# An attention output product on TensorE: stationary operand in four pieces of 32 columns instead of two of 64

## The chip, the cores and the metric

One core of a Trainium2 chip runs the whole program. The metric is device time in microseconds (us), the median of several executions. The core has a matrix engine (TensorE, PE in the profile, with its weight loads listed apart as PEld), VectorE (DVE), ScalarE (ACT), GpSimd (POOL), and DMA queues that SyncE (SP) feeds.

## The reference

The input is a gated linear attention (an mLSTM) over 4 batches, 8 heads, 768 positions and head dimension 40, whose result goes through two feed-forward networks in sequence:

```python
m_new = np.maximum(f_gate[:, :, t] + m, i_gate[:, :, t])
f_stab = np.exp(f_gate[:, :, t] + m - m_new)
i_stab = np.exp(i_gate[:, :, t] - m_new)
C = f_stab * C + i_stab * einsum('bhd,bhe->bhde', vt, kt)
n = f_stab * n + i_stab * kt
y[:, :, t] = sigmoid(o_gate) * einsum('bhde,bhe->bhd', C, qt) / maximum(abs(n . qt), 1)
...
x = y as 3072 tokens x 320
h = (x @ w1) * (x @ w2) @ w3 @ w_out            # first network, width 1024
out = max(h @ w1', h @ w2', h @ w3') @ w_out'   # second network, width 768
```

(Shortened: sizes of axes that only broadcast are left out.)

## The kernel before

**Attention.** The recurrence is worked in chunks of 88 positions (nine to a sequence, the last one of 64). A *unit* is one batch, one chunk and four of the eight heads: 4 x 9 x 2 = 72 units. For each unit TensorE makes the scores of the chunk (L569 or L594), VectorE and GpSimd turn them into a weight tile `pk`, and `outs` (L621 to L629) multiplies `pk` with `kv`. `pk` is the stationary operand: on its 128 partitions stand the 88 positions of the chunk and 40 rows of carried state, and its 128 columns are the 88 output positions and the 40 rows of the next state. `kv` is the moving operand, 41 columns: 40 values and the normalizer. So one product serves outputs and state update, and its result `o` has 128 partitions. In the last chunk there is no next state: its `pk` has 64 columns. For the first chunk the contraction has 88 rows instead of 128.

Both operands are 32-bit floats, and TensorE does each such matmul of the program in two passes: the profile lists two loads and two matmuls for one `PE.matmul` of `outs`.

`outs` cuts the columns of `pk` at multiples of 64, for each of four heads. The two halves write PSUM partitions 0 to 63 and 64 to 127, that is, they lie in different column ranges of the array. That makes 8 matmuls in a unit (4 in a unit of the last chunk), 16 pairs of load and matmul in the profile (8 in the last chunk). A unit's run of them is called a *group* below.

**The networks.** Blocks of 384 tokens go through products with 384 (or 320) moving columns and 128 x 128 stationary operands: `group` (L702 to L706), `b_step` (L769 to L773), `d_step` (L788), and a fold of two weight matrices at the start (L930).

**The order.** All operations are noted in a list, and `Plan.run` replays them with costs per operation and fixed biases to fix the order of each engine ahead of time. The operation that holds a unit's `outs` has a cost of its own there, 910 ns (500 in the last chunk), which is a number in the code and not derived from the matmuls that it holds. Units are spread among the network's steps from about 80 us on.

After `outs`, VectorE reads the result for the next chunk's state (L634) and for the output (L647 to L650).

Of the kernel before, what the change touches and what calls it, by code (L numbers as in the profile page):

```python
# [280 lines left out]
def mlstm_moe_kernel(  # L281
# [55 lines left out]
    o, where, over, gates_done = 0, {}, {t: [] for t, _ in shared}, {}  # L337
# [30 lines left out]
    def T(*key):  # L368
        return made[key]
# [7 lines left out]
    o = 0  # L377
# [30 lines left out]
    def f():  # L408
# [5 lines left out]
         r=[("g", "ff")], w=[("g", "git")])  # L414

    def f():
# [6 lines left out]
         r=[("g", "git")], w=[("g", "aug", 1)])  # L423
# [55 lines left out]
    def ub(u):  # L479
        b, r = divmod(u, 18)  # L480
        return b, r // 2, r % 2, GL[r // 2], 128 if r > 1 else L
# [41 lines left out]
    def unit(u):  # L523
# [48 lines left out]
        else:  # L572
# [19 lines left out]
            def f():  # L592
                for h in range(4):
                    PE.matmul(T("s", u)[0:L, h], lhsT=ks[:, h], rhs=T("qs", u)[:, h], start=True, stop=True)  # L594
                if duo:
                    outs(u - 1)
# [19 lines left out]
        if u + 1 < DUO or u == NU - 1:  # L616
            new(("o", u), [128, 4, 41], F32, f"ac{u % 3}" if u < 10 else "aq")
            P.op("P", 910 if m > n else 500, lambda: outs(u), cols=210, r=[("pk", u), ("kv", u)], w=[("o", u)])
            rest(u)

    def outs(u):  # L621
        b, c, g, n, r = ub(u)
        m = 128 if c < NCH - 1 else n
        for h in range(4):
            for a in range(0, m, 64):
                PE.matmul(  # L626
                    T("o", u)[a:a + 64, h], lhsT=T("pk", u)[:r, h, a:a + 64], rhs=T("kv", u)[:r, h, 40:81],
                    start=True, stop=True,
                )  # L629

# [516 lines left out]
```

## Time and profile before

| | |
|---|---|
| time, median of 3 runs | 722.54 us (722.18 to 725.04) |
| the profiled execution's own time | 725.08 us |
| its span, first to last instruction | 723.1 us |
| TensorE busy | 682.0 us, 94% of the span |
| weight loads busy | 648.9 us, 90% |
| granted TensorE clock, mean over the span | 0.991 of full speed |

Busy time counts each instruction from its start to its modelled end, so instructions that overlap on TensorE are merged and "busy" does not mean at its peak. The times of the section below come from that one execution.

### The profile page before, as it was taken

The page shows a single profiled execution, that of the slowest core. Times are in us where ns is not written, and L with a number is a line of the kernel's source. Part 1 is how long each engine was busy: PE and PEld are TensorE (multiplying, and loading weights), DVE is VectorE, ACT ScalarE, POOL GpSimd, SP SyncE. Part 2 cuts the span into 40 slices and gives each one's busy share as a digit, 9 for nine tenths or more (in the row PEclk, how much of TensorE's full clock was granted, in tenths as well). Part 3 has the DMA queues.
Part 4 walks back from the last instruction along what each step waited for, and adds up shares of the span by engine and source line. Part 5 has one row for each costly group of instructions (what it writes and reads, how often), then busy time and mean ns, then how long its engine had stood idle before and what let it go on. Part 6 is the DMA issues. An engine that isn't in the chain of part 4 may idle for free.

```text
span 723.1 us, 13690 instructions
## 1 busy us (share of the span) xinstructions
PE 682.0 (94%) x4853; PEld 648.9 (90%) x4853; DVE 437.6 (61%) x998; ACT 373.4 (52%) x697; POOL 306.3 (42%) x438
## 2 busy tenths in 40 slices
PE   1569799999999999999999999999999999999998
PEld 1546788889999999999999999999999999999998
DVE  4668877776776865876366666754747632233333
ACT  5859899689864454554343445645333222231311
POOL 1756774566545646674044447643416200000000
PEclk9978999999999999999999999999999999999999
DMA  7987788465433445453033445432305100000000
GB/s 209 249 220 229 225 251 230 141 187 173 137 104 100 101 117 166 120 147 82 9 87 86 110 119 155 122 83 65 88 2 124 39 1 27 1 1 1 1 28 28
DMA packets 50958, 78.91 MB, mean 109 GB/s; under 512 B 11882, under 2 KB 37930, under 8 KB 50890
## 3 DMA queue, kind: packets, MB, share of 16 engines
q1 hardware_dynamic: 50890, 78.04, 39.9%
q8 instruction: 38, 0.62, 0.4%
q14 instruction: 30, 0.25, 0.1%
HBM read 73.98 MB, written 4.03 MB: 108 GB/s over the span
## 4 chain that ended last, share of the span: by engine, by line
PE 78%; ACT 7%; DMA 6%; DVE 3%; issue 2%; POOL 2%; SPq 1%; POOLq 0%; DVEq 0%
PE wk L702 13%; PE wk L704 11%; PE wk L703 11%; PE ac L788 9%; PE wk L706 6%; PE wk L705 6%; PE ac L769 4%; PE aq L626 4%; PE ac L773 4%; PE ac L771 3%; PE wk L930 2%; ACT stg L874 2%; PE aq L594 1%; PE aq L569 1%; DMA qq<-in_qk 1%
## 5 line engine op out<-in xcount | busy, mean ns | idle before, releaser
L722 DVE TENSOR_TENSOR pl<-pr,ph 128x384 fp32r<-128x384 f32 (+1 forms) x91 | 61.1, 672 | 78.3 <-ACT ph L718 74.5
L718 ACT CAST ph<-pr 128x384 fp32r<-128x384 f32 (+1 forms) x114 | 57.8, 510 | 87.1 <-PE ac L788 46.6
L702 PE MATMUL wk<-xh,wch 128*128 128x384 f32 x288 | 99.7, 346 | 0.0
L704 PE MATMUL wk<-xl,wch 128*128 128x384 f32 x288 | 97.0, 337 | 0.0
L703 PE MATMUL wk<-xh,wcl 128*128 128x384 f32 x288 | 97.0, 337 | 0.0
L753 DVE TENSOR_TENSOR pr<-pr,wk 128x384 f32<-128x384 f32 (+1 forms) x98 | 52.9, 541 | 63.4 <-PE wk L706 58.2
L702 PE MATMUL wk<-xh,wah 128*128 128x384 f32 x256 | 90.8, 355 | 0.0
L722 POOL TENSOR_TENSOR pl<-pr,ph 128x384 fp32r<-128x384 f32 (+1 forms) x23 | 23.7, 1033 | 153.9 <-ACT ph L718 136.7
L703 PE MATMUL wk<-xh,wal 128*128 128x384 f32 x256 | 86.1, 336 | 0.0
L704 PE MATMUL wk<-xl,wah 128*128 128x384 f32 x256 | 86.0, 336 | 0.0
L545 POOL TENSOR_TENSOR dd<-am,dd 128x352 f32<-128x352 f32 (+2 forms) x72 | 55.9, 777 | 54.7 <-DMA dd<-d_na 54.0
L559 POOL TENSOR_TENSOR pk<-kv,dd 128x160 f32<-128x160 f32 (+1 forms) x64 | 37.9, 593 | 66.5 <-PE aq L626 59.3
L735 ACT COPY pr<-wk 128x384 f32<-128x384 f32 x64 | 30.5, 476 | 63.3 <-PE wk L706 63.2
L655 POOL TENSOR_TENSOR misc<-misc 88x160 f32<-88x160 f32 (+1 forms) x62 | 44.4, 715 | 41.6 <-DVE misc L650 37.8
L553 ACT ACTIVATE dd<-dd 128x352 f32<-128x352 f32 (+2 forms) x72 | 35.2, 493 | 51.1 <-POOL dd L549 50.4
L737 DVE TENSOR_TENSOR pr<-pr,wk 128x384 f32<-128x384 f32 x64 | 35.2, 550 | 38.7 <-PE wk L706 32.5
L750 ACT COPY pr<-wk 128x384 f32<-128x384 f32 x48 | 23.2, 483 | 68.4 <-PE wk L706 68.3
L874 ACT ACTIVATE stg<-stg 128x512 f16<-128x512 f32 (+2 forms) x41 | 52.7, 1285 | 4.5 <-DVE stg L866 4.0
L702 PEld LDWEIGHTS wk<-xh,wch 128*128 128x128 f32 x288 | 54.1, 188 | 1.0
L703 PEld LDWEIGHTS wk<-xh,wcl 128*128 128x128 f32 x288 | 54.1, 188 | 0.0
L704 PEld LDWEIGHTS wk<-xl,wch 128*128 128x128 f32 x288 | 54.0, 188 | 0.0
L788 PE MATMUL ac<-wd,ph 128*128 128x320 f32 x288 | 51.4, 313 | 0.0
(133 smaller groups left out, 1683.5 us busy)
## 6 DMA issues: line engine op xcount, KB each, us to landing
misc<-in_qk SPq DMA_DIRECT2D x44, 330.0 KB
dd<-d_na SPq DMA_DIRECT2D x56, 176.0 KB
kv<-in_kv SPq DMA_DIRECT2D x72, 121.5 KB
stg<-in_w3t SPq DMA_DIRECT2D x13, 512.0 KB
stg<-in_wc SPq DMA_DIRECT2D x9, 512.0 KB
qq<-in_qk SPq DMA_DIRECT2D x64, 66.0 KB
misc<-in_og SPq DMA_DIRECT2D x31, 120.0 KB
out<-misc SPq DMA_DIRECT2D x23, 160.0 KB
```

What stands on the lines that cost most here:

```text
L545: P.op("G", 735, lambda: G.tensor_tensor(out=T("dd", u)[:r], in0=am[:r, c, h0:h0 + 4].unsqueeze(2).to_broadcast([r, 4, n]), in1=T("dd", u) ...
L655: P.op("G", 485, lambda: G.tensor_tensor(out=yv(), in0=yv(), in1=sg(b, c).rearrange("p (h d) -> p h d", d=D)[:n, g * 4:g * 4 + 4], op=ALU.mult
L702: PE.matmul(p, lhsT=h_[:, kt], rhs=xh[:, kt], start=kt == 0, stop=False)
L703: PE.matmul(p, lhsT=l_[:, kt], rhs=xh[:, kt], start=False, stop=False)
L704: PE.matmul(p, lhsT=h_[:, kt], rhs=xl[:, kt], start=False, stop=False)
L705: PE.matmul(p, lhsT=r_, rhs=xh[:, 2], start=False, stop=False)
L706: PE.matmul(p, lhsT=r_, rhs=xl[:, 2], start=False, stop=True)
L718: P.op("A", act(n), lambda sl=sl: A.copy(out=T("ph", key)[:, sl], in_=T(*src)[:, sl]), r=[src + part], w=[("ph", key) + part])
L722: e.tensor_tensor(out=T("pl", key)[:, sl], in0=T(*src)[:, sl], in1=T("ph", key)[:, sl].bitcast(F32), op=ALU.subtract)
L753: P.op("V", dve(sl.stop - sl.start), lambda ps=ps, sl=sl: V.tensor_tensor(out=T(*sc)[:, sl], in0=T(*sc)[:, sl], in1=T(*ps)[:, sl], op=ALU. ...
L788: PE.matmul(T(f"ac{m}", (k, 1)), lhsT=src[:, m * 128:m * 128 + 128], rhs=w[:, o:o + DM], start=first_, stop=last_,)
L874: A.activation(out=sign, in_=tl()[:, :, 1].bitcast(F32), func=AF.Copy)
```

## The change

The stationary operand is cut at multiples of 32 instead of 64. Nothing else is edited; in particular the cost that the planner uses for the operation stays.

```diff
         for h in range(4):
-            for a in range(0, m, 64):
+            for a in range(0, m, 32):
                 PE.matmul(
-                    T("o", u)[a:a + 64, h], lhsT=T("pk", u)[:r, h, a:a + 64], rhs=T("kv", u)[:r, h, 40:81],
+                    T("o", u)[a:a + 32, h], lhsT=T("pk", u)[:r, h, a:a + 32], rhs=T("kv", u)[:r, h, 40:81],
                     start=True, stop=True,
                 )
```

A unit has now 16 matmuls (8 in the last chunk) with 32 stationary columns each. The order of TensorE's program shows this at a unit between two stretches of the first network; each row is a matmul's line, output, operands and stationary x moving columns, and x16 counts the program's matmuls:

```order
 L706 MATMUL wk_131<-xl_84,war 128x384
 L569 MATMUL aq_133<-misc 88x88 x4
-L626 MATMUL aq_132<-kv_104,pk_97 64x41 x8
+L626 MATMUL aq_132<-kv_104,pk_97 32x41 x16
 L702 MATMUL wk_129<-xh_81,wah 128x384
 L703 MATMUL wk_129<-xh_81,wal 128x384
```

Nothing moved: the group stands between the same neighbours, and this holds for every group. Of the other engines no instruction changed its place either. The program's matmuls of L626 are 544 before and 1088 after, so the pairs of load and matmul in a profile go from 1088 to 2176.

## Rows read from the trace of the kernel before

**Rows 1.** The page: span, TensorE's two rows, granted clock in 40 slices.

```profile
span 723.1 us, 13690 instructions
...
PE 682.0 (94%) x4853; PEld 648.9 (90%) x4853; DVE 437.6 (61%) x998; ACT 373.4 (52%) x697; POOL 306.3 (42%) x438
...
PEclk9978999999999999999999999999999999999999
```

**Rows 2.** Busy time of each engine in three stretches, then granted clock.

```profile
0.00:100.00 100.00, 64.84 (x506) 53.82 (x507) 70.08 (x160) 77.59 (x118) 59.07 (x93) 0.93 0.83 227
100.00:600.00 500.00, 497.34 (x3645) 475.58 (x3644) 327.85 (x764) 266.56 (x518) 243.71 (x342) 1.00 0.41 110
600.00:723.00 123.00, 119.79 (x706) 119.52 (x704) 39.69 (x75) 29.21 (x63) 3.51 (x4) 1.00 0.03 11
```

**Rows 3.** The chain that ended last, by engine and by line (the page).

```profile
PE 78%; ACT 7%; DMA 6%; DVE 3%; issue 2%; POOL 2%; SPq 1%; POOLq 0%; DVEq 0%
PE wk L702 13%; PE wk L704 11%; PE wk L703 11%; PE ac L788 9%; PE wk L706 6%; PE wk L705 6%; PE ac L769 4%; PE aq L626 4%; PE ac L773 4%; PE ac L771 3%; PE wk L930 2%; ACT stg L874 2%; PE aq L594 1%; PE aq L569 1%; DMA qq<-in_qk 1%
```

**Rows 4.** That chain in order of time: start, us, what.

```profile
104.88 0.60 PE aq L626 x16
...
116.14 0.59 PE aq L626 x8
...
306.03 1.98 issue
308.05 0.78 POOL dd L545
308.82 0.90 POOL qs L579
...
584.56 0.59 PE aq L626 x8
```

**Rows 5.** Groups by line and shape: matmuls and loads (xcount, busy us, mean ns).

```profile
L626 PE MATMUL aq<-kv,pk 128*64 128x41 f32 x832 | 37.2, 233 | 2.4 <-DVE misc L650 1.7 <-DVE xl L684 0.5
...
L626 PEld LDWEIGHTS aq<-kv,pk 128*64 128x64 f32 x832 | 30.6, 137 | 8.8 <-issue 2.8 <-DVE misc L650 2.0 <-DVE xl L684 1.1
...
L569 PEld LDWEIGHTS aq<-misc 40*88 40x88 f32 x144 | 12.6, 154 | 8.8 <-issue 2.6 <-DVE pk L610 2.5 <-DVE kv L634 1.7
```

**Rows 6.** Timeline of the weight loads around one full group: start, us, what, xcount.

```profile
168.15 0.19 PEld L706 LDWEIGHTS wk<-xl,war 128*128 128x128 f32 x1
168.59 0.55 PEld L626 LDWEIGHTS aq<-kv,pk 128*64 128x64 f32 x16 [0.25 <-issue]
169.18 0.19 PEld L702 LDWEIGHTS wk<-xh,wah 128*128 128x128 f32 x1
```

**Rows 7.** The last pair of that group: timeline of narrow windows, loads, then matmuls.

```profile
168.99 0.14 PEld L626 LDWEIGHTS aq<-kv,pk 128*64 128x64 f32 x2
...
169.02 0.24 PE L626 MATMUL aq<-kv,pk 128*64 128x41 f32 x2
```

**Rows 8.** Timeline of the loads around a group of the last chunk.

```profile
277.98 0.54 PEld L626 LDWEIGHTS aq<-kv,pk 128*64 128x64 f32 x8
278.56 0.19 PEld L702 LDWEIGHTS wk<-xh,wah 128*128 128x128 f32 x1
```

**Rows 9.** Timelines of two score products L569: 88 stationary columns, moving columns 88, then 64.

```profile
159.13 0.70 PEld L569 LDWEIGHTS aq<-misc 40*88 40x88 f32 x8 [0.25 <-issue]
...
159.13 0.85 PE L569 MATMUL aq<-misc 40*88 40x88 f32 x8
...
111.97 0.70 PEld L569 LDWEIGHTS aq<-misc 40*88 40x88 f32 x8 [0.25 <-issue]
...
111.97 0.83 PE L569 MATMUL aq<-misc 40*88 40x64 f32 x8
```

**Rows 10.** Timelines of folds L930 (32-bit floats, 320 moving columns): one matmul, then 16.

```profile
114.94 0.43 PE L930 MATMUL wk<-wof,w 128*128 128x320 f32 x1
...
159.92 4.58 PE L930 MATMUL wk<-wof,w 128*128 128x320 f32 x16
```

**Rows 11.** Loads of a group at the lower clock, 53.9 to 55.0 us.

```profile
53.94 0.94 PEld L626 LDWEIGHTS ac<-kv,pk 128*64 128x64 f32 x16 [0.20 <-issue]
```

**Rows 12.** DMA queues that fetch instructions (the page, part 3).

```profile
q8 instruction: 38, 0.62, 0.4%
```

## The prediction

> **What bounds the kernel now.** I read the page first. TensorE is busy 94% of a 723.1 us span and its clock is at 0.9 or more in all slices but one [rows 1]. By stretches the picture is sharper: from 100 to 600 us TensorE is busy 497.34 of 500 us, while VectorE has 328 and ScalarE 267 [rows 2]. Before 100 us it is busy only 64.84 of 100, so there it waits for others. The chain that ended last says the same: 78% of it is TensorE [rows 3]. So a microsecond taken from TensorE after 100 us shortens the kernel, unless a wait appears that TensorE's work had covered.
>
> Then the part that changes. In the page's list of the chain L626 has 4% [rows 3]. In the chain in order of time I count 54 of the 72 groups: 46 with x16, which take 0.60 us each, and 8 with x8, which take 0.59 [rows 4]; all but one lie after 100 us. That is 46 x 0.60 + 8 x 0.59 = 32.3 us of chain, and it bounds any gain. The other 18 groups lie beside other work, mostly in the first 100 us.
>
> **How a group spends its 0.60 us.** A group of x16 is eight waves (four heads, two passes), each of two pairs of load and matmul that go to the two column halves. From the loads' row: 0.55 us from the first start to the last end, one load takes 137 ns [rows 5, 6], the second of a wave starts under 10 ns after the first (two loads together take 0.14 us, two matmuls 0.24 [rows 7]; I take 7 ns). So seven intervals between waves take 550 - 137 - 7 = 406 ns: **58 ns a wave**. The remaining 600 - 406 = 194 ns are the last wave and the way to the next group's first load at 169.18 [rows 6]; they do not depend on how often the wave before was repeated.
>
> A group of the last chunk shows what a second column tile costs: it has one pair in a wave, and its eight loads take 0.54 us, (540 - 137) / 7 = 58 ns a wave again [rows 5, 8]. Twice the pairs, in two column ranges, cost the same wave and 0.01 us a group (0.60 against 0.59 [rows 4]). Pairs in different column ranges run side by side.
>
> What sets the 58 ns? Not the matmuls' 41 columns. The score products have 88 stationary columns, and eight of their loads take 0.70 us whether 88 or 64 columns move [rows 9]: (700 - 154) / 7 = 78 ns in both [rows 5]. So with 64 columns moving the stationary side sets the interval, and between 64 and 88 stationary columns it rises by 20 ns for 24 columns, 0.83 ns a column. At the lower clock the same 16 loads take 0.94 us [rows 11]; with a load of 137 to 270 ns that is 95 to 114 ns a wave. The interval follows TensorE's clock, so a queue that hands out instructions at a rate of its own is not what sets it now.
>
> **The change part by part.**
> - *Loads of 32 columns.* By the slope the load side of a wave falls to 58 - 32 x 0.83 = **31 ns**. No row shows a load under 64 columns. Lower bound 31; upper bound 58, if something other than the columns holds it there.
> - *The matmul under it.* The moving side then comes next. The nearest row is the fold, also 32-bit floats: 16 in 4.58 us, one in 0.43, so (4580 - 430) / 15 = 277 ns for 320 columns [rows 10], 0.86 ns a column, so 35 ns for 41. The score product with 88 moving columns needs 78 ns by either side, about 3 ns over 0.86 x 88. I take **38 ns** a wave.
> - *Twice as many pairs.* A wave has four pairs in four column ranges. If each starts 7 ns after the one before, the fourth starts 21 ns after the first and all four fit in 38 ns. The last wave ends 14 ns later than now (7 ns in the last chunk, where one pair becomes two).
> - *Entry and exit.* Before a group the loads sit idle (0.25 us, put down to issue [rows 6]) and behind it the next load comes about 0.19 us after the last wave's. The group has the same neighbours, so both stay.
> - *Instructions.* 1088 more pairs, 2176 more instructions on 13690 [rows 1]. Their fetching is a queue that moves 0.62 MB and takes 0.4% of the DMA engines' time [rows 12]; a fifth more is hidden under a core whose DMA engines are busy 41% after 100 us [rows 2]. Without that cover it would be a stall ahead of some groups; a bound is 0.4% x 723 x 0.2, 0.6 us.
> - *Readers.* VectorE reads `o` after the last matmul, as now, only sooner.
>
> A full group gains 7 x (58 - 38) - 14 = 126 ns, one of the last chunk 140 - 7 = 133 ns. On the chain: 46 x 0.126 + 8 x 0.133 = **6.9 us**. Some comes back: at 306 us the chain leaves TensorE for GpSimd and an issue gap [rows 4], and there are a few such places; TensorE's idle time from 100 to 600 us is 2.7 us [rows 2], and when it runs 7 us ahead these waits grow. I take back about a sixth, 1.1 us, and keep **-5.8 us**. Against the profiled execution's own 725.08 us that is 719.3; on the median of the three runs, which is 2.5 us lower, 722.54 - 5.8 = **716.8 us**. For a reader to weigh other values: each ns on the wave is 7 x 54 = 0.38 us of the kernel. The wave at which nothing changes is 58 - 14/7 = 56 ns.
>
> What a measurement of this kernel can tell from no change is about 0.5%, 3.6 us, that is 67 ns a group: faster by that much needs a wave of 46 ns or less, slower by that much one of 66 ns or more.
>
> **The rivals.**
>
> *The wave does not shrink.* In the last pair the loads start at 168.99 and the matmuls at 169.02 [rows 7]: the matmul follows its load by some 30 ns, and the next load follows that matmul by another 28. If these are fixed lags and not parts of a load's 64 columns, a wave stays at 58 ns and each group loses 14 ns: +0.8 us, 723.3. For it: no row has a load this short. Against it: the interval does grow from 64 to 88 columns. Waves from 47 to 65 ns, by whatever cause, belong here.
>
> *Four are too many at once (the case that ends slower).* The rows show two column ranges side by side, never four. For the second pair to start, its load has to go ahead of the first pair's matmul, which still waits. If only one waiting matmul can be passed, pairs three and four start when the first two are through: a wave becomes two half waves of 38 ns, 76 in all, and the last pair ends 45 ns after the first, against 7 now. A group then costs 7 x 18 + 38 = 164 ns more, +8.9 us on 54 groups: 731.4. It decides from a wave of 66 ns on. For it: twice the pairs in the same queue, and nothing in the trace that is denser than two starts in 58 ns. Against it: from one pair to two, the whole price was 0.01 us a group.
>
> *Each matmul has a least spacing.* If a matmul cannot start less than 25 ns after another on average, a wave of four takes 100 ns, and its last start comes 75 ns after the first: 7 x 42 + 68 = 362 ns a group, +19.5 us, 742. The rows speak for neither side fully: two starts come under 10 ns apart [rows 7], but the mean over a group is 29 ns, which such a limit would allow. The Trainium skill, page "TensorE: Matmul & The Clock Gate", section "Wait — 56ns, not 53.3ns?", states this limit: start to start never drops below about 25 ns however small the moving operand. By that rule the time is the 742 of this rival. The pairs under 10 ns apart disagree with it as a limit for different column ranges, so it gets the smallest chance.
>
> The Trainium skill's page "TensorEngine Tiling (Array Packing)", section "Instruction Overhead", also warns against taking the tiling factor from a dimension that is already small, since a matmul with one moving column takes as long as one with 60. Here the cut is in the stationary columns, and rows 9 show the stationary side setting the interval. If a matmul of 41 columns cost as one of 60, the moving side would be 52 ns at the fold's 0.86 ns a column instead of 35, and the estimate by that page is a gain of some 1.5 us, inside the first rival.
>
> **How the numbers follow.** Forecast (wave 31 to 46 ns) 0.52, its own range 713.5 (31 ns, nothing given back: 7 x 27 - 14 = 175 ns a group, 9.4 us) to 719. The wave does not shrink 0.24, around 723. Four are too many 0.15, around 731. Least spacing 0.09, around 742. The median is that of the likeliest, 716.8. The range from 713.5 to 732 leaves out the last rival and little else. Faster 0.51 (the forecast, but for runs in which the waits eat it); same 0.26; slower 0.23 (the last two).
>
> **What would show it.** In the profile after: L626 with x2176 on TensorE, a full group's 32 loads in about 0.27 + 0.13 = 0.40 us instead of 0.55, the next product 0.47 us after the group's first load instead of 0.60, and the half groups alike; TensorE busy in L626 after 100 us falling by some 7 us, and the idle time between 100 and 600 us up by about a microsecond. I would be wrong if a wave lasts 56 ns or more, which the same row tells; or if the groups shrink and the span does not, and then a wait for GpSimd, ScalarE or a DMA stands in the chain where L626 stood. A change of the clock in the first 100 us, where 0.93 was granted [rows 2], could hide or feign a few us; the clock row tells that apart.

## The result

The changed kernel takes 716.74 us (median of 4 runs, 715.74 to 717.16) against 723.13 us for the kernel before, now with one run more (4 runs, 722.18 to 725.04). The ratio is 0.9906, 95% interval 0.9882 to 0.9930: faster by 6.8 us, between 5 and 8.5. The prediction said 716.8. That is closer than its reasons deserve. It forecast a gain of 5.8 us on a lower median (722.54), and two of its terms were wrong in opposite directions: a group gained 29% more than forecast, and 46 groups counted instead of 54.

The page of the profile after, with the lines that answer to [rows 1, 3, 12] (the profiled execution took 715.74 us):

```profile
span 713.5 us, 15876 instructions
...
PE 672.9 (94%) x5941; PEld 638.5 (89%) x5941; DVE 438.5 (61%) x998; ACT 372.6 (52%) x697; POOL 306.5 (43%) x438
...
PEclk9978999999999999999999999999999999999999
...
q8 instruction: 47, 0.77, 0.5%
...
PE 75%; ACT 8%; DMA 6%; DVE 4%; POOL 3%; issue 2%; SPq 2%; POOLq 0%; ACTq 0%; DVEq 0%
```

There are 1088 pairs of load and matmul more, TensorE's busy time is 9 us shorter, and the chain that ended last has given up 3 points of TensorE, mostly to ScalarE, VectorE and GpSimd. The clock row reads the same. The span is 9.6 us shorter while the medians differ by 6.4: the profiled execution of before took 725.08 us, more than any of the four timed ones, and some 2 us of the difference between the two traces lie ahead of 105 us. The runs' own spread covers that: one of the runs below, with TensorE's program as before up to there, reaches the same group as early.

The stretches, to set beside [rows 2]:

```profile
100.00:600.00 500.00, 496.38 (x4557) 474.74 (x4556) 328.33 (x768) 266.51 (x520) 242.29 (x340) 1.00 0.42 110
```

TensorE's idle time from 100 to 600 us went from 2.7 to 3.6 us. So it is as full as it was, and it finishes earlier.

The loads around the group that answers to [rows 6], then the one of the last chunk that answers to [rows 8] (start, us, what, xcount):

```profile
167.55 0.38 PEld L626 LDWEIGHTS aq<-kv,pk 128*32 128x32 f32 x32 [0.25 <-issue]
167.98 0.19 PEld L702 LDWEIGHTS wk<-xh,wah 128*128 128x128 f32 x1
...
275.72 0.37 PEld L626 LDWEIGHTS aq<-kv,pk 128*32 128x32 f32 x16
276.14 0.19 PEld L702 LDWEIGHTS wk<-xh,wah 128*128 128x128 f32 x1
```

One load takes 110 ns now:

```profile
L626 PEld LDWEIGHTS aq<-kv,pk 128*32 128x32 f32 x1664 | 21.1, 110 | 9.3 <-DVE misc L650 3.1 <-issue 1.9 <-DVE xl L684 1.2
```

The reader reads a wave from it as before: (380 - 110 - 20) / 7 = **36 ns** (predicted 38, before 58). From the group's first load to the next product's it is 167.98 - 167.55 = **0.43 us** (predicted 0.47, before 0.60), and 0.42 in the last chunk. The idle 0.25 us ahead of the group is unchanged.

### The profile page after: what moved, and what is told of

Same layout as the page of the kernel before. It is cut to its first block, busy times and chain, and to the rows that moved or that the text cites. A ratio compares the mean times of both kernels' runs of the same rounds, so it can differ in the third digit from the quotient of the medians.

```text
span 713.5 us, 15876 instructions
## 1 busy us (share of the span) xinstructions
PE 672.9 (94%) x5941; PEld 638.5 (89%) x5941; DVE 438.5 (61%) x998; ACT 372.6 (52%) x697; POOL 306.5 (43%) x438
## 4 chain that ended last, share of the span: by engine, by line
PE 75%; ACT 8%; DMA 6%; DVE 4%; POOL 3%; issue 2%; SPq 2%; POOLq 0%; ACTq 0%; DVEq 0%
PE wk L702 13%; PE wk L703 12%; PE wk L704 12%; PE ac L788 9%; PE wk L706 6%; PE wk L705 6%; PE ac L769 4%; PE ac L773 4%; PE aq L626 3%; ACT stg L874 3%; PE ac L771 3%; DMA kv<-in_kv 2%; DMA stg<-in_wo 2%; PE aq L594 2%; DMA stg<-in_w3t 2%
## 5 line engine op out<-in xcount | busy, mean ns | idle before, releaser
L655 POOL TENSOR_TENSOR misc<-misc 88x160 f32<-88x160 f32 (+1 forms) x62 | 42.5, 685 | 44.4 <-DVE misc L650 39.7
```

Source lines behind the costliest of these rows:

```text
L655: P.op("G", 485, lambda: G.tensor_tensor(out=yv(), in0=yv(), in1=sg(b, c).rearrange("p (h d) -> p h d", d=D)[:n, g * 4:g * 4 + 4], op=ALU.mult
```

## What the experiments asked

The theory is that of the prediction: a wave lasts as long as the slower of two sides, the loads (0.83 ns for each stationary column, and 5) and the moving columns (0.86 ns each, and 1 to 3), and pairs in different column ranges run side by side. The rivals: stationary columns alone set the wave; the way in and out of the divided array is what counts; the order in the queue does not matter. A second question is where along the kernel a shorter group counts. Six of the runs have one timed execution each (both with 81 moving columns, the pieces of 21 and 20, the two orders of the queue, both widths in one group). They are read by their traces; a difference of one or two us between their times shows nothing.

**No cut, 128 columns.** (Below, only the loop in `outs` is edited where nothing else is said; lines with - are those of the changed kernel.)

```diff
-            for a in range(0, m, 32):
-                PE.matmul(T("o", u)[a:a + 32, h], lhsT=T("pk", u)[:r, h, a:a + 32], ...)
+            PE.matmul(T("o", u)[:m, h], lhsT=T("pk", u)[:r, h, 0:m], ...)
```

> The operand is not cut at all: one matmul of 128 stationary columns a head (64 in the last chunk). Theory (a wave lasts as long as the slower of its load side, 0.83 ns a stationary column and 5, and its moving side, 0.86 ns a moving column; column ranges run side by side): a wave of 0.83 x 128 + 5 = 112 ns, seven intervals 0.78 us, and since the array is not divided the loads need not sit idle before and behind a group; a group with its way in and out some 0.2 us longer than with two of 64, about 11 us on 54 groups: 733 us (728 to 738). Rival (the way in and out of the divided array is what costs, and waves stay near 58 ns): a gain of 0.2 us a group, about 712.

730.41 us, ratio to before 1.0097 (1.0059 to 1.0135): 7 us slower. The loads of a full group:

```profile
225.29 0.97 PEld L625 LDWEIGHTS aq<-kv,pk 128*128 128x128 f32 x8
226.19 0.19 PEld L701 LDWEIGHTS wk<-xh,wch 128*128 128x128 f32 x1
```

With 192 ns for one load, (970 - 192) / 7 = 111 ns a wave, against 112 by the line through 64 and 88 columns. There is no idle time ahead of the group, but that pays back only a part. So the load side is shown at 64, 88 and 128 columns, and the rival with the way in and out is out.

**81 moving columns**, with four of 32 and with two of 64. The product takes the keys along (`rhs=T("kv", u)[:r, h, 0:81]`, `o` is 81 columns wide), and its readers use the last 41. The run with two of 64 is edited from the kernel before.

> Four of 32 columns, and 81 moving columns instead of 41 (the keys go through the product as well; only the 41 columns used before are read). Theory: the moving side sets the wave now, 0.86 x 81 + 1 to 3 = 71 to 73 ns, where 41 columns gave 36; a full group about 0.25 us longer than in the changed kernel, 13 us in all: about 730. Rival (the wave of 36 ns is set by the 32 stationary columns): 36 ns, 717 us.

> Two of 64 columns, and 81 moving columns instead of 41. Theory: a wave of 71 to 73 ns by the moving side, the same as with four of 32, against 58 by the load side with 41 moving columns; group 0.09 to 0.10 us longer than before, 5 us in all: about 728, and no more than 2 us from the run with four of 32. Rival (stationary columns set the wave): 58 ns, 723 us.

729.76 and 730.32 us. The loads, of four of 32:

```profile
176.36 0.58 PEld L626 LDWEIGHTS aq<-kv,pk 128*32 128x32 f32 x32 [0.25 <-issue]
177.07 0.19 PEld L702 LDWEIGHTS wk<-xh,wah 128*128 128x128 f32 x1
```

and of two of 64:

```profile
174.83 0.62 PEld L626 LDWEIGHTS aq<-kv,pk 128*64 128x64 f32 x16 [0.25 <-issue]
175.55 0.19 PEld L702 LDWEIGHTS wk<-xh,wah 128*128 128x128 f32 x1
```

0.71 and 0.72 us: with 81 moving columns the cut is worth nothing, since the moving side sets both waves. Read as above, a wave is (580 - 110 - 20) / 7 = 64 ns and (620 - 137 - 7) / 7 = 68 ns. That is under the expected 71 to 73 because the first interval of a group is short (29 and 55 ns); from the second on it is 69 to 75 ns in both. That is the other half of the theory, and it puts the limit of this change: it pays as long as the loads are the slower side.

**41 moving columns in two pieces of 21 and 20**, to bring the loads back on top.

```diff
         for h in range(4):
-            for a in range(0, m, 32):
+            for x, y in ((0, 21), (21, 41)):
+                for a in range(0, m, 32):
```

> Four of 32 columns with the moving operand in two pieces of 21 and 20 columns: 64 pairs in a full group, 16 waves. Theory: a wave is set by its loads now, 0.83 x 32 + 5 = 31 to 32 ns, fifteen intervals 0.47 us, the group 0.66 us against 0.43: +12 us, about 729. Rival 1 (the moving side sets it throughout): 20 ns a wave, 0.49 us, about 720. Rival 2 (the 36 ns are four starts of 9 ns each, a limit of the queue): 36 ns a wave, 0.73 us, about 733.

731.77 us, and in the trace:

```profile
175.36 0.64 PEld L627 LDWEIGHTS aq<-kv,pk 128*32 128x32 f32 x64 [0.25 <-issue]
176.03 0.19 PEld L703 LDWEIGHTS wk<-xh,wah 128*128 128x128 f32 x1
```

(640 - 110 - 20) / 15 = 34 ns a wave and 0.67 us a group, against 0.66 by the theory, 0.49 and 0.73 by the rivals. The moving side alone (20 ns) is out. The mean of 34 lies between the loads' 31 and the queue's 36, but the first half of the group tells them apart. Its 32 loads are as many as a whole group of the changed kernel has (there 0.38 us):

```profile
175.36 0.35 PEld L627 LDWEIGHTS aq<-kv,pk 128*32 128x32 f32 x32 [0.25 <-issue]
```

(350 - 113 - 20) / 7 = 31 ns a wave, with 113 ns for one of these loads and four starts in each wave. So the loads set it, and a limit of the queue at 36 ns is out. In the second half the four ranges fall out of step, which makes the mean longer.

**The order of the queue.** The column range outside, the head inside:

```diff
-        for h in range(4):
-            for a in range(0, m, 32):
+        for a in range(0, m, 32):
+            for h in range(4):
```

> The same 32-column matmuls as in the changed kernel, the column range in the outer loop and the head in the inner one, so that the next pairs in the queue go to the same range. Theory: pairs of one range can't overlap and matmuls start in order, so a full group is 32 waves of 31 to 38 ns with one pair each, about 1.2 to 1.3 us instead of 0.43; on 54 groups some 45 us: about 760 us. Rival (the queue pulls later pairs ahead, or fewer columns alone made the gain): the order doesn't matter, 717 us.

737.96 us. The order matters (21 us), but the group is not the 1.2 to 1.3 us of pairs one by one:

```profile
174.69 0.90 PEld L626 LDWEIGHTS aq<-kv,pk 128*32 128x32 f32 x32 [0.25 <-issue]
175.64 0.19 PEld L702 LDWEIGHTS wk<-xh,wah 128*128 128x128 f32 x1
```

0.95 us. The single records show why the theory was too strict: pairs of one range start 36 ns apart, but the next range begins about 180 ns after the first one. Up to that moment, 174.87, six loads and five matmuls have started:

```profile
174.69 0.29 PEld L626 LDWEIGHTS aq<-kv,pk 128*32 128x32 f32 x6 [0.25 <-issue]
...
174.69 0.37 PE L626 MATMUL aq<-kv,pk 128*32 128x41 f32 x5
```

So three of the first range's eight matmuls still wait. (The records do not name the range; from there on two rows of starts run side by side, and the new one is known by its short first interval of 28 ns.) So a range seems to take up to about three waiting pairs, and what stands behind them can go ahead into another range. That gave a test, the same loops for two heads at a time, four pairs in a row instead of eight:

```diff
-        for h in range(4):
-            for a in range(0, m, 32):
+        for g2 in (0, 2):
+            for a in range(0, m, 32):
+                for h in (g2, g2 + 1):
```

> The 32-column matmuls in another order: for two heads at a time, all of one column range before the next, so four pairs in a row go to the same range (eight in a_outer, two in the changed kernel). In a_outer the second range started after 180 ns, with three pairs of the first still to come, and a full group took 0.95 us instead of 1.2 to 1.3. Theory: a range can hold about three waiting pairs, so four in a row let all ranges run side by side and the group takes 0.43 to 0.48 us, as in the changed kernel: 717 to 720 us. Rival (ranges overlap only at the seams between runs of the same range, in proportion to the runs' length): 0.6 to 0.7 us, about 727 to 731.

714.03 us (one run; its first 90 us were 2 to 3 us shorter than in the trace of the changed kernel, so it is no better kernel by this). The group:

```profile
170.30 0.42 PEld L627 LDWEIGHTS aq<-kv,pk 128*32 128x32 f32 x32 [0.25 <-DVE stg L881]
170.77 0.19 PEld L703 LDWEIGHTS wk<-xh,wah 128*128 128x128 f32 x1
```

0.47 us, as the theory of three waiting pairs says, not 0.6 to 0.7.

**Both widths in one group**, two of 64 for three heads and four of 32 for the last (`w = 32 if h == 3 else 64`).

> Two of 64 columns for three heads, four of 32 for the last. Theory: the way out of a group follows the columns of its last matmuls, so the next group's load comes 126 ns after the last matmul's start, as with four of 32, and not 158 as with two of 64. The two widths meet inside a group; if going from one to the other empties the array like going from the undivided one, the group has a gap of about 0.1 us and takes about 0.63 us (725 us), if not, 0.53 us (720 us). Rival (the way out follows something else, such as the number of pairs in the group): 158 ns.

726.97 us. The loads of the 64s, and, in a later window, of the 32s:

```profile
173.74 0.43 PEld L627 LDWEIGHTS aq<-kv,pk 128*64 128x64 f32 x12 [0.25 <-issue]
...
174.22 0.16 PEld L627 LDWEIGHTS aq<-kv,pk 128*32 128x32 f32 x8
...
174.43 0.19 PEld L703 LDWEIGHTS wk<-xh,wah 128*128 128x128 f32 x1
```

Going from 64 to 32 columns inside a group costs a gap: the last load of the 64s starts near 174.03 and the first of the 32s at 174.22, as long a way as from a group of 64s to the next undivided product. The group takes 0.69 us, more than before. The way out came 138 ns after the last matmul's start, neither 126 nor 158, so the expectation was not met as put. Counted from the last load's start it is 0.16 us, as with four of 32 throughout, against 0.19 with two of 64 [rows 6, 7]: with 41 moving columns the way out is a last wave and a rest of 129 ns both times (165 - 36, 187 - 58). It is not a fixed rest in general: with 81 moving columns the next product's load comes 231 ns after the last one, about 160 over a wave of 71. What the rest follows is not shown.

**Where along the kernel it counts.** The cut at 32 in the first 28 units alone (`w = 32 if u < DUO else 64`), and in units 28 to 71 alone (`u >= DUO`).

> Four of 32 only in the first 28 units (those up to about 210 us), two of 64 in the others. Theory (a group's gain counts only where TensorE's own queue ends last, which in these traces is after about 210 us): the first 28 groups get 0.16 us shorter each, 4.6 us in all, but little of it shows: 722 us (721 to 723.5). Rival (every group on the chain gives its gain): about 718.5.

> Four of 32 only in units 28 to 71, two of 64 in the first 28. Theory: nearly the whole gain, 38 x 0.163 + 6 x 0.169 = 7.2 us of TensorE's time, less about a microsecond that waits take back: 716.5 us (715.5 to 717.5). Rival (every group gives its gain): about 718.5, two thirds of the gain.

Early: 722.30 us, ratio 0.9978 (0.9958 to 0.9998). Late: 718.10 us, ratio 0.9934 (0.9912 to 0.9957). Both were compared with the same runs of the kernel before (median 724.16). By ratios that is 1.6 us (0.1 to 3.0) and 4.8 us (3.1 to 6.4); the rival put both at 718.5, a gain of 4 to 5 us each. The early part gives a little more than expected, and its interval leaves the rival out. The late part gives less: 718.10 lies outside the expected 715.5 to 717.5 and nearer to the rival, and the interval of its gain holds both.

The traces are sharper. The stretch from the group at 104.81 us of the kernel before to the one at 206.97 holds eleven groups; TensorE's busy time stands behind the length:

```profile
104.81:206.97 102.16, 101.99 (x689) 89.54 (x688) 76.12 (x167) 87.75 (x143) 57.80 (x73) 1.00 0.57 169
...
102.77:205.60 102.83, 102.05 (x688) 89.57 (x687) 77.09 (x167) 87.70 (x143) 59.36 (x74) 1.00 0.58 170
...
102.07:204.23 102.16, 100.44 (x849) 87.75 (x848) 76.08 (x167) 87.84 (x143) 58.14 (x73) 1.00 0.61 171
...
102.79:205.92 103.13, 100.60 (x848) 87.77 (x847) 77.06 (x167) 87.99 (x144) 58.12 (x73) 1.00 0.58 170
```

These are the kernel before, late, early and the changed kernel. Late has the long groups here and the changed kernel the short ones; they enter the stretch 0.02 us apart, and the changed kernel leaves it 0.3 us later. Its TensorE works 1.45 us less and waits 1.75 us more. In early, too, the shorter groups turn into waiting (1.72 us, against 0.17 in the kernel before). So in these traces, one of each kernel, the cut gives nothing in this stretch. Behind it, up to the last group, the traces gain 1.2 us (early, three short groups there), 6.7 (late, 43) and 8.4 (the changed kernel, 46) on the kernel before.

**The planner told of shorter groups** (1210 to 1050, 910 to 750, 500 to 330 ns in the operations' costs), the one candidate for something better than both. The 1210 is the operation in which, from unit 27 on, `outs` runs together with the next unit's scores; the 910 and 500 of the section on the order hold for the units ahead of that, and for the very last.

> The changed kernel with the planner told of the shorter groups: its costs for the operations that hold them go down by 160 ns (1210 to 1050) and 160 and 170 ns (910 to 750, 500 to 330). No matmul changes, only the order that the planner finds. Theory: TensorE's work is the same, and its idle time after 210 us is 1 us, so an order can gain little there; the biases were fitted to the old costs, so it may lose: 717 us, within 4 us either way. Rival (the old costs make units come later than they could): 713 or less.

730.20 us, ratio 1.0106 (1.0089 to 1.0123): 8 us slower than before and outside the 4 us expected. Its TensorE is busy 681.8 us instead of 672.9 and was granted 0.88 of its clock in the first 100 us and 0.95 from 100 to 210, against 0.91 and 1.00 in the changed kernel. So the new order leaves TensorE waiting early (from 100 to 210 us it is busy 103.38 of 110 us, against 107.47) and part of the work runs at the lower clock; which operation comes late there was not followed. None of these kernels is shown to be faster than the changed one.

## Why the prediction held

*What bounds the kernel:* right for the stretch behind 207 us, but not ahead of it, and the prediction did not draw that limit. (The granted clock is under 0.9 in two slices of [rows 1], not one.) It counted 54 groups on the chain, 10 of them between 100 and 210 us. The chain of the kernel after has two in that stretch:

```profile
198.32 0.43 PE aq L626 x32
206.00 0.43 PE aq L626 x32
```

What stands there instead, from 145 to 150 us, where before there was TensorE's own work (first row):

```profile
148.74 4.31 PE wk L930 x16
...
145.79 1.38 ACT stg L874
147.19 0.69 DVE stg L880
147.88 1.17 DVE stg L866
149.13 1.36 ACT stg L874
```

That is the splitting of the weights on ScalarE and VectorE, a second chain that was nearly as long. TensorE now waits for VectorE, on which that chain runs: in the stretch of eleven groups shown above the idle time ahead of the score products L569, for VectorE each time, goes from 0.2 us (first row, before) to 2.4 (after):

```profile
L569 PE MATMUL aq<-misc 40*88 40x88 f32 (+1 forms) x81 | 8.7, 246 | 0.2 <-DVE pk L610 0.2
...
L569 PE MATMUL aq<-misc 40*88 40x88 f32 (+1 forms) x81 | 8.7, 246 | 2.4 <-DVE misc L650 1.2 <-DVE kv L634 0.7 <-DVE pk L610 0.6
```

Before, the group at 104.88 and the last one at 584.56 [rows 4] are 479.7 us apart; after, 472.3. From 104.88 to the group at 207.04 (after, at 206.00) the kernel after even takes 1.0 us longer (it had entered 2 us earlier); from there on it gains 8.4 us. Between those two groups lie 46, on the chain or beside it; by 0.163 to 0.169 us they make 7.5, and for the 0.9 more see 306 us below. So 46 groups count, not 54. The chain that ended last names what is on the path; it does not say how far behind the next chain is.

*The wave:* right. 36 ns, set by the moving side; the 31 for the loads under it were measured with the pieces of 21 and 20.

*The rest of the group:* wrong, and this is the term that was mis-sized. The prediction kept 194 ns and added 14 for the later starts. Measured, the part ahead of the first load is the same, but the part behind the last load start went from 0.19 to 0.16 us: the last wave is in it, and at 41 moving columns it shrinks like the others. So a full group gained 0.163 us instead of 0.126, and one of the last chunk 0.169 instead of 0.133. Of the 37 ns, some 22 are the way out and 14 the wave (36 ns instead of 38, seven times). The prediction's 6.9 us came from more groups at a smaller gain each; that its sum is near the 7.5 us of 46 groups is luck, and so is the closeness of 716.8, which also has the 1.1 us below in it. The interval of the measured gain, 5 to 8.5 us, holds 5.8, 6.9 and 7.5 alike. The lower end of the range is a small slip: 722.54 less 9.4 is 713.1, not 713.5.

*What comes back:* 1.1 us were taken off for waits. TensorE's idle time from 100 to 600 us did grow by 0.9 us, but what was lost was lost before 207 us, and not in the places that the prediction named. Near 306 us the chain still leaves TensorE, with issue gaps of under half a microsecond where 1.98 us stood [rows 4]. From the group at 207 us to the last one, before and after:

```profile
206.97:584.49 377.52, 375.92 (x2832) 367.77 (x2831) 242.63 (x578) 171.09 (x359) 180.54 (x259) 1.00 0.38 96
...
205.92:575.06 369.14, 368.05 (x3527) 359.99 (x3526) 241.34 (x578) 170.46 (x359) 179.78 (x259) 1.00 0.39 98
```

TensorE is idle 1.60 us before and 1.09 after, so there 0.5 of the 0.9 us were won; the rest was not followed.

*Instructions:* 0.15 MB more in nine packets, and at the group shown above no stall ahead of it that was not there.

*The rivals:* a wave that does not shrink is out at 36 ns. Four at once are not too many. A least spacing of 25 ns is out for different column ranges: four starts in 36 ns are 9 ns on average over a whole group. The Trainium skill's rule that start to start never drops below about 25 ns ("TensorE: Matmul & The Clock Gate", section "Wait — 56ns, not 53.3ns?") therefore disagrees with this trace where the matmuls go to different column ranges. Another section of that page of the Trainium skill, "LDWEIGHTS (loading the stationary operand)", gives a load 1/1.2 ns for each column. The intervals between loads in the traces agree with its slope, 58 ns at 64 columns, 78 at 88 and 111 at 128, about 5 ns over it each.

## What to carry to other kernels

Where small matmuls come in rows, find which side sets their spacing, stationary or moving columns, by two rows that differ in one of them; here, cutting the stationary operand into column ranges paid until the moving side was reached, and the order has to bring other ranges near (four pairs in a row to one range cost a group 0.04 us, eight 0.52). A group's end holds a wave too: take the last one into the sum. And before a gain is multiplied by the groups on the chain, ask in each stretch what the next longest chain is; a run with the change in one part alone shows it.

## What was not expected of the hardware

Pairs behind others that wait for their column range go ahead into another range: in the order with eight in a row the next range started with three still waiting, and with four in a row a group lost only 0.04 us. Changing from 64 to 32 columns inside a group cost a gap of about 0.19 us between loads, as leaving the divided array does. Four ranges of 32-bit float loads and matmuls of 41 columns ran side by side with starts 7 ns apart and no loss over one: 36 ns for a wave of four, and 36 ns from pair to pair within one range.
